# Joining the sign of decoded weights: bit operation on VectorE instead of sign and product on ScalarE and GpSimd

## Chip, core and metric

The kernel runs on one core of one Trainium2 chip. The metric is device time in microseconds, the median of several executions. The engines are called as in the profile: PE (TensorE, with its weight loads as PEld), DVE (VectorE), ACT (ScalarE), POOL (GpSimd) and SP (SyncE, which issues all of this kernel's transfers).

## What is computed

Attention over 8 batches of 8 heads (576 positions, 64 per head), in which only scores within tau of a row's maximum count, and behind it two matrix products with a gate between them:

```python
scores = scale * np.matmul(q, k.transpose(0, 1, 3, 2))
thresh = np.max(scores, axis=-1, keepdims=True) - tau
scores = np.where(scores >= thresh, scores, -1000000000.0)
...
out = np.matmul(attn, v)                     # per head; heads are joined to x, 4608 x 512
...
h = x @ w_in                                 # w_in 512 x 2048
g = h * (1.0 / (1.0 + np.exp(-h)))
return (g @ w_out).astype(np.float32)        # w_out 2048 x 512
```

The weights `w_in` and `w_out` are handed over as 64-bit floats. A 64-bit float is two 32-bit words here, a low and a top one; sign, exponent and the first 20 bits of the mantissa are in the top word.

## The kernel before, in words

Attention runs tile by tile: 128 query rows of one head against all 576 keys. For each tile PE computes scores (`scores`, L400 for the first, direct visits, L412 after), DVE takes the row maximum (L422), ACT the exponential (L429), DVE the threshold and row sum (L441, L445, L449), ACT scales (L454). The result is split into a high and a low half-precision part (ACT L463 or POOL L465, POOL L468 and L471), transposed by DMA (L481) and multiplied with v on PE (L496). In the first visits, which cover the first 256 rows of each head of batch 0, PE transposes instead (L357, L359), and L377 multiplies with v. K and q are split as well (ACT L324, L310, L315; POOL L326, L311; DVE L316). Once a batch's rows are there, units of the two matrix products are put between the attention tiles: `h_unit` (PE L530, then ACT L538, DVE L539, ACT L546, DVE L547) and `o_unit` (PE L562, ACT L572).

The weights are made once, in 32 tiles of 128 x 512, 16 of `w_in` and then 16 of `w_out`. `load_weights` has SP fetch a tile's words (L169): eight of the `w_in` tiles into parts of `gbuf`, all others into `wraw`, a pool of two buffers that are used in turn, so a load waits until all readers of the tile two before it are done. `decode_weights` turns a tile's words into 32-bit floats in `wst`:

- POOL L179 reads the top words as floats and scales them, which moves the exponent into its place but three bits to the right;
- DVE L183 shifts the words left by three, which drops the sign, and L186 joins the top three bits of the low words;
- PE L197 adds up the tile's columns in four matmuls with ones, which needs the magnitudes without sign, and for every fourth tile DVE L202 takes the maximum of the sums;
- ACT L204 takes the sign of the top words into a half-precision tile `wsg` (two buffers), and POOL L205 multiplies `wst` with it in place. POOL therefore waits for L186, for L197's reading of the tile, and for L204.

When the 16 tiles of a matrix are decoded, `pow2_scales` makes a scale from the maxima, and `split_weights` splits each tile into two half-precision parts (ACT L211, DVE L212) in place, one row of `wst` further down. Matrix products wait for these parts.

The program is written in the order of attention tiles; `W_PLAN` says at which tile each load, decode and split is put, the second group with a raised priority. A planner then sorts the instructions of each engine by priority and by its own estimate of when they are ready. Each engine works off its own queue in that fixed order. SP's queue, which issues the loads of weights, of q, k and v, and the transposes, stands still when the transfer at its head has to wait.

Of the kernel before, what the change touches and what calls it, by code (L numbers as in the profile page):

```python
# [9 lines left out]
F16 = mybir.dt.float16  # L10
BF16 = mybir.dt.bfloat16
F32 = mybir.dt.float32
F32R = mybir.dt.float32r
I32 = mybir.dt.int32
AF = mybir.ActivationFunctionType
ALU = mybir.AluOpType
# [3 lines left out]
P = 128  # L20
# [32 lines left out]
def attention_moe(  # L53
# [10 lines left out]
    nc = tc.nc  # L64
# [5 lines left out]
    stage = stage_ctx.enter_context(tc.tile_pool(name="stage", bufs=2))  # L70
# [7 lines left out]
    def bank(shape, name, own=None):  # L78
        if own is None:
            own = turn[0] = (turn[0] + 1) % turn[1]  # L80
        return ps_m.tile(shape, F32, tag=f"m{own}", name=name)
# [7 lines left out]
        out=gate, in0=tau_sb, scalar1=0.0, scalar2=0.125, op0=ALU.is_ge, op1=ALU.mult  # L89
# [3 lines left out]
        out=ntau, in0=tau_sb, scalar1=0.0, scalar2=-1.0, op0=ALU.max, op1=ALU.mult  # L93
# [55 lines left out]
    ident = const.tile([P, P], F32, name="ident")  # L149
    make_identity(nc, ident)  # L150
    wsc = {}

    w_words = (w_in.bitcast(I32), w_out.bitcast(I32))
    wraw = {}
    wps = {}
# [16 lines left out]
    def decode_weights(i):  # L172


        t = wraw.pop(i)
        low, top = t[:, :, 0], t[:, :, 1]
        w = wst[:, i + WSPARE, :]
        wbits = w.bitcast(I32)
        nc.gpsimd.tensor_scalar(  # L179
            out=w, in0=top.bitcast(F32), scalar1=2.0**-112, scalar2=1.0,  # L180
            op0=ALU.mult, op1=ALU.mult,
        )
        nc.vector.tensor_scalar(  # L183
            out=wbits, in0=wbits, scalar1=3, scalar2=None, op0=ALU.logical_shift_left
        )
        nc.vector.scalar_tensor_tensor(  # L186
            out=wbits, in0=low, scalar=29, in1=wbits,
            op0=ALU.logical_shift_right, op1=ALU.bitwise_or,
        )


        n, c = divmod(i, 4)
        if c == 0:
            wps[n] = bank([P, P], f"wps_{n}", 2)
        upper = w.bitcast(BF16).rearrange("p (c t) -> p c t", t=2)[:, :, 1]
        for j in range(4):
            nc.tensor.matmul(  # L197
                wps[n], ones, upper[:, j * P : (j + 1) * P],
                start=(c == 0 and j == 0), stop=(c == 3 and j == 3),
            )  # L200
        if c == 3:
            nc.vector.tensor_reduce(out=wmx[:, n : n + 1], in_=wps[n], op=ALU.max, axis=AX.X)  # L202
        sg = stage.tile([P, 512], F16, tag="wsg", name=f"wsg_{i}", bufs=2)
        nc.scalar.activation(sg, top.bitcast(F32), AF.Sign)  # L204
        nc.gpsimd.tensor_tensor(out=w, in0=w, in1=sg, op=ALU.mult)  # L205

    def split_weights(i):
        w = wst[:, i + WSPARE, :]
# [452 lines left out]
    for first, t0, t1, t2, hp in W_PLAN:  # L661
        for i in range(16):
            ti = t0 + i * (t1 - t0) / 16
            at(math.floor(ti - 2), pri(hp, lambda i=i + first: load_weights(i)))
            at(math.floor(ti), pri(hp, lambda i=i + first: decode_weights(i)))
        at(t1, pri(hp, scale_out if first else scale_in))
        for i in range(16):
            at(t1 + i * (t2 - t1) // 16, pri(hp, lambda i=i + first: split_weights(i)))
# [116 lines left out]
```

## Time and profile before

| | |
|---|---|
| median of 3 runs | 1275.36 us (1275.25 to 1276.07) |
| the profiled execution | 1276.61 us, its span 1274.6 us |
| PE busy | 1155.0 us, 91% of the span |
| DVE busy | 940.2 us, 74% |
| ACT busy | 869.0 us, 68% |
| POOL busy | 754.1 us, 59% |
| granted TensorE clock, mean | 0.969 |

Busy times are of one profiled execution, counted from its first to its last instruction. The sum of a forecast is made against that execution's own time; the median of the other runs lies 1.25 us below it. A share of the span mixes stages: the first 154 us, in which the weights are decoded beside the first attention tiles, look different from the rest, so the rows below separate them. A row that groups instructions gives busy time, mean duration of one, and the idle time of the engine just before them. DVE instructions overlap a little with the one behind them, so a start-to-start distance can be shorter than a duration.

### The profile page before, as it was taken

How to read it: one execution, taken by the hardware profiler on the slowest of the kernel's cores; microseconds unless marked ns; L12 is line 12 of the kernel's file. 1: busy time of each engine (PE TensorE's matmuls, PEld its weight loads, DVE VectorE, ACT ScalarE, POOL GpSimd, SP SyncE). 2: the span in 40 equal slices, each digit the busy share in tenths (PEclk: the TensorE clock that was granted, in tenths of full speed). 3: DMA queues.
4: the chain of work that ended last, by engine and by line, in shares of the span. 5: the costliest groups of instructions: out<-in, count | busy, mean ns of one | idle time of the engine just before them, and what ended most of it. 6: DMA issues, size and time to landing. Idle time of an engine off the chain costs nothing.

```text
span 1274.6 us, 27048 instructions
## 1 busy us (share of the span) xinstructions
PE 1155.0 (91%) x9400; PEld 897.5 (70%) x9400; DVE 940.2 (74%) x2339; ACT 869.0 (68%) x1793; POOL 754.1 (59%) x952
## 2 busy tenths in 40 slices
PE   5766669899899899998989999999989999999998
PEld 3544558567677677776767777787777777777777
DVE  7899997987987988868588767977597847521431
ACT  6887877787787877867478746877488747532431
POOL 5568979687788777884478608872578508300000
PEclk9886989899899999999999999999999999999999
DMA  9456778778698778782678528781687518400000
GB/s 303 133 173 165 166 135 156 153 134 179 138 158 159 149 159 154 137 166 67 140 135 151 121 75 159 141 161 50 129 158 138 111 24 139 73 15 20 6 15 19
DMA packets 363480, 158.15 MB, mean 124 GB/s; under 512 B 329552, under 2 KB 338256, under 8 KB 363344
## 3 DMA queue, kind: packets, MB, share of 16 engines
q1 hardware_dynamic: 363344, 156.43, 59.5%
q8 instruction: 74, 1.21, 0.4%
q14 instruction: 62, 0.51, 0.1%
HBM read 66.72 MB, written 9.44 MB: 60 GB/s over the span
## 4 chain that ended last, share of the span: by engine, by line
PE 47%; DVE 22%; POOL 9%; issue 9%; ACT 6%; DMA 6%; SPq 1%; POOLq 0%; ACTq 0%; DVEq 0%
PE o L562 20%; PE h L530 14%; PE s L412 6%; DVE w L441 6%; PE a L496 6%; DVE sm L422 4%; DMA wT<-hl 4%; POOL hl L468 3%; DVE qstack L316 3%; POOL hl L465 3%; DMA vraw<-in_vL 2%; ACT w L429 2%; DVE wst L212 2%; DVE gbuf L547 1%; ACT w L454 1%
## 5 line engine op out<-in xcount | busy, mean ns | idle before, releaser
L530 PE MATMUL h<-x,wst 128*128 128x288 f16 (+2 forms) x3072 | 416.2, 291 | 20.8 <-DVE gbuf L547 16.9
L562 PE MATMUL o<-gbuf,wst 128*128 128x288 f16 (+2 forms) x3072 | 398.8, 287 | 0.1
L530 PEld LDWEIGHTS <-wst 128*128 128x128 f16 x3072 | 295.0, 99 | 111.6 <-issue 29.5
L562 PEld LDWEIGHTS <-wst 128*128 128x128 f16 x3072 | 292.5, 98 | 83.7 <-issue 6.7
L468 POOL TENSOR_TENSOR hl<-w,hl 128x512 f16<-128x512 f32 x272 | 324.5, 1193 | 13.5
L465 POOL TENSOR_SCALAR hl<-w 128x576 f16<-128x576 f32 x264 | 182.8, 696 | 238.6 <-ACT w L454 127.4
L429 ACT ACTIVATE w<-s,sm 128x576 f32<-128x576 f32 x288 | 213.1, 740 | 99.8 <-DVE sm L422 32.6
L441 DVE SCALAR_TENSOR_TENSOR w<-s,sm,w 128x576 f32<-128x576 f32 x288 | 233.5, 812 | 61.9 <-ACT sm L433 28.9
L422 DVE TENSOR_REDUCE sm<-s 128x1 f32<-128x576 f32 x288 | 216.4, 752 | 70.3 <-PE s L412 66.0
L454 ACT ACTIVATE w<-w,sm 128x576 f32<-128x576 f32 x288 | 220.4, 773 | 52.1 <-DVE sm L449 50.5
L412 PE MATMUL s<-khi,qstack 128*128 128x288 f32 x608 | 157.0, 340 | 52.3 <-DVE w L441 49.1
L539 DVE SCALAR_TENSOR_TENSOR h<-th,h 128x288 f32<-128x288 f32 (+2 forms) x256 | 116.3, 456 | 81.4 <-ACT th L538 76.0
L412 PEld LDWEIGHTS s<-khi,qstack 128*128 128x128 f32 x608 | 96.1, 193 | 81.4 <-issue 46.1
L538 ACT ACTIVATE th<-h,msc 128x288 f32<-128x288 f32 (+2 forms) x256 | 127.8, 502 | 26.8 <-PE h L530 24.4
L547 DVE SCALAR_TENSOR_TENSOR gbuf<-h,gbuf 128x288 f16<-128x288 f32 (+2 forms) x256 | 115.3, 452 | 37.6 <-ACT gbuf L546 36.8
L546 ACT ACTIVATE gbuf<-h 128x288 f16<-128x288 f32 (+2 forms) x256 | 104.6, 410 | 50.9 <-DVE h L539 50.3
L496 PE MATMUL a<-wT,v 128*64 128x288 f16 (+1 forms) x1680 | 127.8, 293 | 8.3 <-DMA wT<-hl 7.1
L412 PE MATMUL s<-klo,qstack 128*128 128x288 f32 x608 | 132.9, 299 | 0.0
L326 POOL TENSOR_TENSOR klo<-kraw,khi 128x576 fp32r<-128x576 f32 x64 | 93.0, 1453 | 43.7 <-ACT khi L324 43.7
L496 PEld LDWEIGHTS <-v 128*64 128x64 f16 x1680 | 90.7, 111 | 36.0 <-issue 20.9
L412 PEld LDWEIGHTS s<-klo,qstack 128*128 128x128 f32 x608 | 99.8, 192 | 1.1 <-issue 1.1
L471 POOL TENSOR_TENSOR hl<-w,hl 128x64 f16<-128x64 f32 x272 | 99.7, 367 | 0.0
(84 smaller groups left out, 915.1 us busy)
## 6 DMA issues: line engine op xcount, KB each, us to landing
qraw<-in_qT SPq DMA_DIRECT2D x128, 144.0 KB, 3.0
kraw<-in_kT SPq DMA_DIRECT2D x128, 144.0 KB, 3.0
vraw<-in_vL SPq DMA_DIRECT2D x32, 320.0 KB, 3.8
wraw<-in_w_out SPq DMA_DIRECT2D x16, 512.0 KB, 4.2
out_t<-wst SPq DMA_DIRECT2D x56, 144.0 KB, 2.4
wT<-hl SPq DMA_TRANSPOSE x304, 3.3
gbuf<-in_w_in SPq DMA_DIRECT2D x8, 512.0 KB, 6.8
wraw<-in_w_in SPq DMA_DIRECT2D x8, 512.0 KB, 4.9
```

The costliest lines, as they stand in the source:

```text
L412: nc.tensor.matmul(s_ps[:, j, :HALF], lhs, kk[:, j * HALF : (j + 1) * HALF], start=(n == 0), stop=(n == len(seq) - 1),)
L422: nc.vector.tensor_reduce(out=negm, in_=s_ps[:, :, :HALF], op=ALU.max, axis=AX.XY, negate=True)
L429: nc.scalar.activation(wtile[t].rearrange("p (j c) -> p j c", j=2), sps[t][:, :, :HALF], AF.Exp, bias=small[t][:, 0:1],)
L441: nc.vector.scalar_tensor_tensor(out=w3, in0=s_ps[:, :, :HALF], scalar=sm[:, 1:2], in1=w3, op0=ALU.is_ge, op1=ALU.mult, accum_out=sm[:, 2:3],)
L454: nc.scalar.activation(w, w, AF.Copy, scale=r)
L465: nc.gpsimd.tensor_scalar(out=fl[:, 0:S], in0=w, scalar1=1.0, scalar2=1.0, op0=ALU.mult, op1=ALU.mult)
L468: nc.gpsimd.tensor_tensor(out=fl[:, 640:1152], in0=w[:, 0:512], in1=fl[:, 0:512], op=ALU.subtract)
L496: nc.tensor.matmul(a_ps[odd * D : (odd + 1) * D, :n], vt[:, lo_v, odd, kv, :], wT[v, b * H + 2 * p + odd][:, kw, c0 - base : c0 - base + n ...
L530: nc.tensor.matmul(ph[:, :n], wi(c, f, lo_w), x16[b, lo_x][:, c, c0 : c0 + n], start=(k == 0), stop=(k == 11),)
L538: nc.scalar.activation(th[:, :n], ph[:, :n], AF.Tanh, scale=moe_sc[b][:, 0:1])
L547: nc.vector.scalar_tensor_tensor(out=g[:, 1, :n], in0=ph[:, :n], scalar=2.0**-14, in1=g[:, 0, :n], op0=ALU.mult, op1=ALU.subtract,)
L562: nc.tensor.matmul(ps[:, :n], wo(f, d, lo_w), g[:, lo_g, :n], start=(f == 0 and k == 0), stop=(f == NF - 1 and k == 2),)
```

## The change

The sign of a tile is no longer computed as a number. One DVE instruction takes the top words, keeps bit 31 of each, and joins it with the magnitudes in `wst` by a bitwise or, in place. ACT's L204 and POOL's L205 go, and with them the tile `wsg`. The new instruction stands at the same place of `decode_weights`, behind the four matmuls that read the magnitudes and behind L202. It reads the raw top words, which L204 read before. What `wst` holds at the end is the same. (One empty line goes as well, so that lines between it and the new instruction move up by one.)

```diff
-        sg = stage.tile([P, 512], F16, tag="wsg", name=f"wsg_{i}", bufs=2)
-        nc.scalar.activation(sg, top.bitcast(F32), AF.Sign)
-        nc.gpsimd.tensor_tensor(out=w, in0=w, in1=sg, op=ALU.mult)
+        nc.vector.scalar_tensor_tensor(
+            out=wbits, in0=top, scalar=-(2**31), in1=wbits,
+            op0=ALU.bitwise_and, op1=ALU.bitwise_or,
+        )
```

## Rows read from the trace of the kernel before

**Rows 1.** Busy us (and instructions) of PE, PEld, DVE, ACT, POOL; clock; DMA
```profile
6.00:100.00 94.00, 67.59 (x335) 43.30 (x335) 87.06 (x191) 75.40 (x156) 53.72 (x51) 0.86 0.62 203
100.00:154.00 54.00, 32.35 (x230) 24.90 (x229) 51.26 (x104) 41.25 (x82) 49.39 (x50) 0.81 0.76 176
...
154.00:1274.00 1120.00, 1055.07 (x8836) 829.32 (x8836) 801.05 (x2039) 750.78 (x1555) 649.34 (x844) 0.99 0.59 115
```

**Rows 2.** Pieces of the chain of waits: start us, us, what
```profile
14.19 1.30 POOL wst L205
...
145.21 0.10 POOL wst L205
...
1108.40 21.67 PE o L562 x176
```

**Rows 3.** Instructions by line: shortest/median/longest ns, first and last start in us
```profile
L183 DVE TENSOR_SCALAR wst<-wst x32: 403/762/1375, 11.9 to 146.0; 128x512 int32<-128x512 int32 x32
...
L186 DVE SCALAR_TENSOR_TENSOR wst<-wraw,wst x24: 676/692/1827, 24.1 to 147.3; 128x512 int32<-128x512 int32 x24
...
L212 DVE SCALAR_TENSOR_TENSOR wst<-wst,i_w_sc x16: 729/1054/1906, 77.6 to 128.1; 128x512 f16<-128x512 f32 x16
...
L205 POOL TENSOR_TENSOR wst<-wst,wsg x32: 1144/1163/1682, 14.2 to 153.1; 128x512 f32<-128x512 f32 x32
```

**Rows 4.** Groups by line, 0 to 154 us: busy us, mean ns | idle before, releaser
```profile
L183 DVE TENSOR_SCALAR wst<-wst 128x512 int32<-128x512 int32 x32 | 26.5, 830 | 3.1 <-POOL wst L179 3.1
...
L186 DVE SCALAR_TENSOR_TENSOR wst<-wraw,wst 128x512 int32<-128x512 int32 x24 | 20.3, 848 | 0.0
L212 DVE SCALAR_TENSOR_TENSOR wst<-wst,i_w_sc 128x512 f16<-128x512 f32 x16 | 18.1, 1130 | 0.0
L186 DVE SCALAR_TENSOR_TENSOR wst<-gbuf,wst 128x512 int32<-128x512 int32 x8 | 8.0, 1003 | 0.0
...
L205 POOL TENSOR_TENSOR wst<-wst,wsg 128x512 f32<-128x512 f32 x32 | 40.6, 1275 | 22.4 <-PE wps L197 14.0 <-ACT wsg L204 2.3 <-issue 1.7
...
L204 ACT ACTIVATE wsg<-wraw 128x512 f16<-128x512 f32 x24 | 16.0, 665 | 5.8 <-DMA wraw<-in_w_out 4.4 <-POOL wst L205 1.5
```

**Rows 5.** Timeline, DVE and POOL: start us, us, instruction [idle before, releaser]
```profile
41.65 0.68 DVE L186 SCALAR_TENSOR_TENSOR wst<-gbuf,wst 128x512 int32<-128x512 int32 x1
42.25 0.81 DVE L441 SCALAR_TENSOR_TENSOR w<-s,sm,w 128x576 f32<-128x576 f32 x1
...
45.97 2.27 POOL L205 TENSOR_TENSOR wst<-wst,wsg 128x512 f32<-128x512 f32 x2 [9.45 <-PE wps L197]
```

**Rows 6.** Timeline, the first and the last of 18 pairs of POOL and DVE
```profile
18.89 1.16 POOL L205 TENSOR_TENSOR wst<-wst,wsg 128x512 f32<-128x512 f32 x1 [1.73 <-issue]
19.30 1.03 DVE L183 TENSOR_SCALAR wst<-wst 128x512 int32<-128x512 int32 x1
...
145.21 1.16 POOL L205 TENSOR_TENSOR wst<-wst,wsg 128x512 f32<-128x512 f32 x1
146.01 0.65 DVE L183 TENSOR_SCALAR wst<-wst 128x512 int32<-128x512 int32 x1
```

**Rows 7.** Timeline, POOL and DVE behind one line 205
```profile
107.10 1.15 POOL L205 TENSOR_TENSOR wst<-wst,wsg 128x512 f32<-128x512 f32 x1
...
108.22 1.33 POOL L468 TENSOR_TENSOR hl<-w,hl 128x512 f16<-128x512 f32 x1
...
108.46 1.64 DVE L212 SCALAR_TENSOR_TENSOR wst<-wst,i_w_sc 128x512 f16<-128x512 f32 x1
```

**Rows 8.** Waits of DVE up to 155 us: us in total, times, longest us
```profile
DVE vmx L239 <- DMA vraw<-in_vL: 5.0, 4, 3.3
DVE wst L183 <- POOL wst L179: 3.1, 4, 1.9
```

**Rows 9.** Waits of POOL and of SP's queue up to 155 us
```profile
POOL wst L205 <- PE wps L197: 14.0, 3, 9.5
...
SPq L169 <- DVE wst L186: 27.9, 12, 4.7
```

## Prediction

> **What bounds the kernel now.** The page's shares show PE as the fullest engine over the whole run, but that is an average over stages. So I went on to the busy time by stretch, where the reader should compare the columns within a row. From 154 us on, PE works 1055.07 of 1120 us: it sets the pace there. From 6 to 100 us it works only 67.59 of 94 us and from 100 to 154 only 32.35 of 54 [rows 1]. Another engine is full there: DVE is busy 87.06 and 51.26 us of these two stretches, so that from 6 to 154 us it idles 9.7 us in all. POOL is a little over half busy up to 100 us (53.72 of 94) and nearly full after (49.39 of 54) [rows 1]. The weights are decoded in just this stretch: the first line 205 starts at 14.2, the last at 153.1 us [rows 3]. A DVE queue that is almost never empty, and on which the softmax that feeds PE stands in order, is the bound of this stage.
>
> Does a delay there reach the end? The chain of waits ends in a backlog that PE works off in blocks of 21 to 24 us from 1108 us on [rows 2]. PE's order is fixed in the program, and this backlog stands behind the attention of the last batch. What the first stage loses is therefore lost at the end: PE could win back only idle time after 154 us (65 us of 1120 [rows 1]), and no row says that a late start fills it.
>
> **How full is DVE really?** Its busy time includes being held. The shortest line 183 takes 0.403 us and the mean is 0.830; line 186 takes 0.676 at the shortest against 0.848 and 1.003; line 212 takes 0.729 against 1.130 [rows 3, 4]. Over 32, 24 + 8 and 16 instructions that is 13.7 + 6.7 + 6.4 = 26.8 us above the shortest forms. The timeline shows by what: POOL runs nothing for the 9.45 us before 45.97 us, and line 186 stands at its shortest there [rows 5]; but while line 205 runs on POOL from 18.89 us for 1.16, line 183 starts at 19.30 and ends at 20.33, 0.3 us behind it, having taken 1.03 [rows 6]. I paired each long DVE instruction of these three lines with the POOL instruction that it overlaps most. 18 of them fall to line 205, the first at 19.30 and the last at 146.01 us [rows 6], 12.9 us together.
>
> **The change part by part.**
> 1. Removed from POOL: 32 of line 205, 40.6 us, mean 1.275 [rows 4]. POOL isn't the fullest engine of the stage, so this is no gain by itself; the gain is what line 205 holds DVE, at most 12.9 us. After 100 us POOL is so full that its next instruction moves up into the place: behind the line 205 of 107.10 stands line 468 at 108.22, which holds line 212 for 1.64 us [rows 7]. I therefore count 9 of the 12.9; the ends are 6, about half, and 12.9.
> 2. Removed from ACT: 32 of line 204, of which 24 took 16.0 us [rows 4]. ACT is busy 75.40 of 94 and 41.25 of 54 us [rows 1], and neither of DVE's two longest waits of the stage is for it [rows 8]. I count nothing, since DVE's own queue covers it; without that cover a tile's chain would be shorter by nothing either, because line 204 reads the raw words and can run beside lines 179 to 197. The far end is the 21 us that all 32 take at 0.665 each, if ACT were the bound.
> 3. Added to DVE: 32 bit operations. The trace has their like: line 186, the same kind of instruction on the same tile, one strided input and one in place, 128x512 words, 0.676 us [rows 3]. The instruction behind it starts 0.60 us after it (41.65 to 42.25) [rows 5]. 32 x 0.60 = 19.3 us, on the fullest engine. To this comes what POOL's remaining work holds them. Line 186 loses 6.7 / 32 = 0.21 each now, 3.2 us of it in the pairs with line 205, which leaves 0.11 each, 3.5 us. The ends are nothing and line 212's 0.40 each, 12.8 us. I take 3.5, by the row of its own kind.
> 4. A new wait. The operation rewrites the tile that line 197's four matmuls read, so DVE now waits for PE where POOL did. Behind it on DVE stand softmax and the next decode, for which PE's scores wait. POOL stands 14.0 us in three such waits, the longest 9.5 [rows 9]; that one is POOL's empty time before 45.97 us [rows 5]. A planner orders DVE's queue and may place the operation after other work. The ends are 0 and 14 us; I take 3, nearer to nothing because 29 of the 32 had no such wait.
> 5. Load buffers. Tiles outside gbuf rotate through two buffers, freed so far by lines 179, 186 and 204, then by line 179 and the added operation, which comes after PE. SP's queue already stands 27.9 us behind line 186 for such loads, with the transposes and the q and k loads behind them [rows 9]. A late load would show on DVE through POOL's line 179, for which line 183 waits 3.1 us in all [rows 8]. That is the far end of this step, and I put it inside the 3 us of step 4.
> 6. DVE's idle 9.7 us can take part of the new work. 5.0 of it are waits for v from memory [rows 8], which need not end earlier. I take 4; the ends are 0 and 9.7.
>
> The sum is 19.3 + 3.5 - 9 + 3 - 4 = +12.8 us. The profiled execution took 1276.61 us around its span of 1274.6; the median of the runs, 1275.36, lies 1.25 below it. 1276.6 + 12.8 - 1.25 gives 1288.
>
> One rule speaks against step 3. Line 186 has two inputs of 32 bits from SBUF and takes 0.676 us at its shortest [rows 3]. The Trainium skill, "Vector Engine (DVE) Microarchitecture Reference", section "Points that are easy to get wrong", puts this form of instruction at half throughput when both inputs lie in SBUF and aren't bf16. At the 1.0417 ns a column that the same page gives at full rate, half rate would add some 0.53 us to each, 17 us in all, an estimate from that page, and the sum would be +30. The trace doesn't agree: 0.676 us leaves only 0.14 beside 512 columns at full rate.
>
> **The rivals.**
> A, faster: POOL is the real limit after 100 us. For it: POOL's 49.39 of 54 us [rows 1], and line 205 as a link of the chain of waits, seven times from 14.19 to 145.21 us, 7.9 us together [rows 2]. Then all 12.9 us of holds go, the other 13.9 shrink with POOL's busy time (103 to some 63 us, 38%: 5.3), the chain drops its 7.9, and part of DVE's idle is filled as before: 19.3 + 3.5 - 12.9 - 5.3 - 7.9 - 4 = -7 us, 1268. It decides if POOL ends last after 100 us. Against it: DVE is fuller than POOL in the same stretch, 51.26 to 49.39 us [rows 1]. The Trainium skill sides with this rival in "GPSIMD Engine Reference", section "Engine selection": elementwise work with two inputs belongs on VectorE, GpSimd being about twice as slow. The trace agrees on the ratio (1.144 to 0.676 us at the shortest [rows 3]).
> B, slower than the forecast: DVE waits for PE as POOL did, 14.0 us in place of the 3, and, standing, fills none of its idle: 12.8 + 11 + 4 = +28, 1303. It decides where the operation stands at the head of DVE's queue while PE still works through scores.
> C, it cancels: all 12.9 us of holds go and all of DVE's idle is filled, 19.3 + 3.5 - 12.9 - 9.7 = 0, 1275. This needs every wait of DVE to be one that the new work can fill; half of the idle is for memory.
> That the planner sorts other instructions anew when a step costs something else is in no row. It can move each case by some us either way, and I take nothing for it.
>
> **How the numbers follow.** The forecast, +6 to +20 us around 1288, gets 0.50, because DVE's load grows by an amount that rows give. A gets 0.20, B 0.18, C 0.12. About 0.2% (2.6 us) is what a measurement of this kernel can tell from no change. Faster by more than that is A, 0.20; within it C, 0.12; slower the forecast and B, 0.68. The range 1266 to 1303 takes in A's and B's own times and leaves about 0.1 out on each side, where their further ends lie.
>
> **What would show it.** The added operation should have a mean of 0.7 to 0.9 us; above 1 us step 3 is wrong. Line 183's mean should fall from 0.83 to some 0.55; if it stays, step 1 is wrong. The last line 183, which started at 146.0 us [rows 6], should come some 13 us later, with DVE over 90% busy until then; well below 90% and earlier is A. The block that PE begins at 1108 us [rows 2] should begin later by as much; if not, later stages give time back, and the passage to the end was wrong. DVE's waits for PE at the new operation tell the forecast (about 3 us) from B (over 10).

## The result, and the profile after

The changed kernel takes 1283.85 us (median of 4 runs, 1281.78 to 1285.09) against 1275.71 before: ratio 1.0050, 95% interval 1.0027 to 1.0073, about 6 us by the ratio (the two medians lie 8.1 us apart). Run once more it came to 1.0061 (1.0039 to 1.0083), about 8 us. The change makes the kernel slower, by some 6 to 8 us. The profiled execution has a span of 1283.3 us. Lines have moved: 169, 179, 183, 186 and 197 are 168, 178, 182, 185 and 196 now, line 202 is the added operation and the column maximum is line 201.

Groups of VectorE instructions of the changed kernel up to 200 us (busy us, mean ns | idle before, releaser); rows 4 holds the same of before:

```profile
L182 DVE TENSOR_SCALAR wst<-wst 128x512 int32<-128x512 int32 x32 | 20.4, 636 | 4.7 <-POOL wst L178 4.7
L202 DVE SCALAR_TENSOR_TENSOR wst<-wraw,wst 128x512 int32<-128x512 int32 x24 | 19.9, 831 | 0.0
L185 DVE SCALAR_TENSOR_TENSOR wst<-wraw,wst 128x512 int32<-128x512 int32 x24 | 19.8, 830 | 0.0
L212 DVE SCALAR_TENSOR_TENSOR wst<-wst,i_w_sc 128x512 f16<-128x512 f32 x16 | 14.9, 935 | 0.0
...
L202 DVE SCALAR_TENSOR_TENSOR wst<-gbuf,wst 128x512 int32<-128x512 int32 x8 | 6.0, 766 | 0.0
```

The added operation has a mean of 0.831 and 0.766 us, as line 185 beside it. Line 182 fell from 0.830 to 0.636 and line 212 from 1.130 to 0.935 [rows 4]: GpSimd holds VectorE less. And the added operation has no idle time before it: VectorE did not stand waiting for PE there (only the column maximum, just ahead of it, waits 1.8 us for PE, 0.8 before).

Busy time by stretch, columns as in rows 1:

```profile
6.00:100.00 94.00, 67.75 (x346) 43.75 (x347) 84.41 (x199) 62.39 (x130) 27.24 (x29) 0.82 0.60 183
100.00:154.00 54.00, 32.60 (x237) 25.69 (x236) 49.85 (x107) 38.55 (x82) 39.36 (x43) 0.81 0.82 178
```

VectorE is no busier in these two stretches than before (84.41 and 49.85 us against 87.06 and 51.26 [rows 1]), although it has a new operation. So the work is not squeezed into the same time; it is spread. The maxima of the column sums show over what (shortest/median/longest ns, first and last start in us), first of before, then of the changed kernel:

```profile
L202 DVE TENSOR_REDUCE wmx<-wps x8: 265/278/292, 26.3 to 148.7; 128x1 f32<-128x128 f32 x8
```

```profile
L201 DVE TENSOR_REDUCE wmx<-wps x8: 274/278/292, 27.2 to 193.3; 128x1 f32<-128x128 f32 x8
```

The decode ends at 193.3 us instead of 148.7. Attention, meanwhile, is ahead: line 441, which each softmax tile passes once, ends for the 33rd time at 161.3 us instead of 171.7, for the 57th time at 242.0 instead of 253.9, and is late only at the 65th (285.5 against 277.1). PE was ahead as well at 154 us, with 583 matmuls since 6 us instead of 565 (the counts in the two rows above and in rows 1). But at 242 us it is behind, with 1035 matmuls since the start instead of 1116: the softmax of the 57th tile is early because units of the two matrix products have been put behind it (378 matmuls of lines 530 and 562 by 242.0 us, against 492 by 253.9). PE loses its lead from 200 to 230 us (columns as in rows 1, first before, then the changed kernel):

```profile
200.00:230.00 30.00, 28.59 (x250) 24.50 (x248) 22.91 (x68) 22.14 (x43) 24.72 (x34) 1.00 0.90 181
```

```profile
200.00:230.00 30.00, 22.18 (x130) 15.87 (x130) 29.84 (x62) 26.32 (x47) 29.33 (x31) 0.83 0.71 133
```

Of the matmuls in these 30 us, 90 instead of 152 are of line 562, which needs `w_out`. The splits of `w_out` (line 212) start from 199.5 to 229.3 us instead of 151.5 to 186.1, on a VectorE that is busy for 29.84 of the 30 us. Waits of PE between 200 and 260 us in the changed kernel:

```profile
PE o L562 <- DVE wst L212: 4.6, 5, 1.6
PE s L412 <- DVE w L441: 3.0, 5, 1.3
```

Before, line 562 doesn't wait for line 212 in this stretch, and PE is busy for 53.79 of the 60 us, now for 49.51. From there on a delay stays: 6.2 us at the 121st line 441 (459.1 against 452.8), and PE's backlog begins at 1117.08 us instead of 1108.40 [rows 2], 8.7 us later, which is the difference of the two spans.

```profile
1117.08 21.67 PE o L562 x176
```

**Why the decode is late.** The raw words of a tile are now free only when the sign is in, and there are two buffers. Timeline of the changed kernel, one buffer's turns (start us, us, what):

```profile
145.72 0.54 SPq L168 DMA_DIRECT2D wraw<-in_w_out  x1
...
160.18 0.35 SPq L168 DMA_DIRECT2D wraw<-in_w_out  x1
...
175.28 0.54 SPq L168 DMA_DIRECT2D wraw<-in_w_out  x1
```

```profile
155.93 1.51 DVE L185 SCALAR_TENSOR_TENSOR wst<-wraw,wst 128x512 int32<-128x512 int32 x1
159.28 0.87 DVE L202 SCALAR_TENSOR_TENSOR wst<-wraw,wst 128x512 int32<-128x512 int32 x1
...
174.22 0.68 DVE L202 SCALAR_TENSOR_TENSOR wst<-wraw,wst 128x512 int32<-128x512 int32 x1
```

The load issued at 145.72 fills a buffer; line 185 has used its low words by 157.44; the sign ends at 160.15, and 0.03 us later the next load into that buffer is issued. The sign of that tile ends at 174.90, and the next load stands at 175.28. A buffer turns once in about 15 us, so two of them let one tile through in 7.5. That is the pace of the whole of `w_out`: the last 16 tiles' line 185 starts from 79.9 to 190.8 us, 7.4 us a tile. Before, line 186 of these tiles started from 71.2 to 147.3 us, 5.1 us a tile. GpSimd shows the same from the other side; its waits up to 200 us, changed kernel:

```profile
POOL wst L178 <- DMA wraw<-in_w_out: 27.4, 11, 5.7
POOL wst L178 <- DMA wraw<-in_w_in: 20.0, 7, 15.0
POOL wst L178 <- DMA gbuf<-in_w_in: 17.6, 7, 9.5
```

Before, these were 8.0, 2.3 and 9.3 us. A GpSimd that has lost its product waits for loads.

### The profile page after: what moved, and what is told of

Its sections match the earlier page's. It is cut to its first block, busy times and chain, and to the rows that moved or that the text cites. A ratio compares the mean times of both kernels' runs of the same rounds, so it can differ in the third digit from the quotient of the medians.

```text
span 1283.3 us, 26993 instructions
## 1 busy us (share of the span) xinstructions
PE 1159.9 (90%) x9400; PEld 898.9 (70%) x9400; DVE 949.9 (74%) x2371; ACT 853.5 (67%) x1761; POOL 717.9 (56%) x920
## 4 chain that ended last, share of the span: by engine, by line
PE 44%; DVE 23%; POOL 10%; issue 9%; ACT 6%; DMA 5%; SPq 1%; POOLq 0%; ACTq 0%; DVEq 0%
PE o L562 18%; PE h L530 15%; DVE w L441 6%; PE s L412 5%; PE a L496 5%; DVE sm L422 4%; POOL hl L468 4%; DMA wT<-hl 3%; DVE qstack L316 3%; POOL hl L465 3%; ACT w L429 2%; POOL hl L471 2%; DVE wst L212 1%; DVE gbuf L547 1%; ACT w L454 1%
```

## Experiments

Two theories went in. D: the loss is the load of 32 more operations on a full VectorE, minus what taking line 205 away gives back. L: the loss is the longer hold of the raw words, which paces the decode of `w_out`. Times are given as ratios to the kernel before on the same chip, with 95% intervals, and in us as the ratio's share of 1277 us.

**The product on VectorE, the raw words freed early** (on the kernel before):

```diff
-        nc.gpsimd.tensor_tensor(out=w, in0=w, in1=sg, op=ALU.mult)
+        nc.vector.tensor_tensor(out=w, in0=w, in1=sg, op=ALU.mult)
```

> The kernel before with line 205's product moved from GpSimd to VectorE; ScalarE still takes the sign, so the raw words are released early, as before. VectorE gets 32 operations with two SBUF inputs, as in the change, and the same wait for PE. Theory L (the loss of the change comes from the raw words being held longer, so that the two load buffers pace the decode of w_out): the last column maximum comes back to 150 to 160 us and the time to 1271 to 1279 us. Theory D (the loss comes from 32 more operations on a full VectorE): 1283 us or more, as the change or worse, since ScalarE keeps its work.

1.0018 (0.9995 to 1.0041), +2 us, and the column maxima end at 163.6 us. The same load and the same place on VectorE as in the change (mean 0.879 us), without the hold: the decode ends 30 us earlier than in the change, though still 15 later than before and 4 later than L expected. The expected time of L was right at its upper end, D's was too high. The step from here to the change is 4 to 6 us, with intervals that overlap, so its size isn't certain.

**The hold alone** (on the kernel before; `held` is one column):

```diff
+    held = const.tile([P, 1], F32, name="held")
...
         nc.gpsimd.tensor_tensor(out=w, in0=w, in1=sg, op=ALU.mult)
+        nc.gpsimd.tensor_tensor(
+            out=held[:, 0:1], in0=w[:, 0:1], in1=top[:, 0:1].bitcast(F32), op=ALU.mult
+        )
```

> The kernel before, with one GpSimd operation of one column added behind line 205 of each tile that reads the raw words and the finished tile: the load buffer is held until the sign is in, and nothing else changes (32 operations of 0.1 to 0.3 us on GpSimd). Theory L: the last column maximum comes 20 to 45 us later than at 149 us, and the time rises by 4 to 12 us, to 1280 to 1288. Theory D: 1275 to 1278 us, the decode ends at 149 to 155 us.

1.0142 (1.0115 to 1.0170), +18 us, more than L expected, and the column maxima end at 236.1 us, 87 later than before, where L expected 20 to 45:

```profile
L203 DVE TENSOR_REDUCE wmx<-wps x8: 272/278/293, 25.5 to 236.1; 128x1 f32<-128x128 f32 x8
```

GpSimd's product comes later than the change's operation on VectorE, so the buffers are held longer still. The added column takes about 0.19 to 0.36 us, 32 of them some 7 us on an engine that isn't full; they don't explain an end 87 us later. Nor does attention show a fuller engine in the first stage: its 33rd softmax tile is early (150.2 us against 171.7), its 65th late (303.0 against 277.1), as in the change. A hold can cost more than the whole change.

**The load alone** (on the kernel before, behind line 186):

```diff
+        nc.vector.scalar_tensor_tensor(
+            out=wbits, in0=wbits, scalar=0, in1=wbits,
+            op0=ALU.logical_shift_right, op1=ALU.bitwise_or,
+        )
```

> The kernel before with 32 more VectorE operations of the form of line 186 (the tile joined with itself, which leaves it as it is) right behind line 186: the VectorE load of the change alone, without the wait for PE, without the longer hold, with ScalarE and GpSimd as before. Theory D: +12 to +25 us, 1288 to 1300, since line 205 still holds VectorE too. Theory L: +0 to +5 us.

1.0140 (1.0112 to 1.0168), +18 us, where D expected 12 to 25 and L at most 5. VectorE is full from 100 to 154 us (columns as in rows 1):

```profile
100.00:154.00 54.00, 26.78 (x173) 19.45 (x172) 54.00 (x98) 39.93 (x76) 42.08 (x39) 0.72 0.67 159
```

Here attention is late from the first stage on: line 441's work ends for the 33rd time at 184.1 us instead of 171.7, for the 57th at 272.6 instead of 253.9. The added operation also stands ahead of PE's reading of the tile, and the column maxima end at 182.9 us with the raw words freed as before: a late decode by itself doesn't point to the hold. So neither theory is the whole: each cause alone costs 18 us on the kernel before.

**No sign at all** (the change without its operation; the weights stay magnitudes):

```diff
-        nc.vector.scalar_tensor_tensor(
-            out=wbits, in0=top, scalar=-(2**31), in1=wbits,
-            op0=ALU.bitwise_and, op1=ALU.bitwise_or,
-        )
```

> The change without the added operation: no sign is joined on any engine, so the weights stay magnitudes. It prices what taking away lines 204 and 205 gives by itself. Both theories: faster than before; by the prediction's step 1 some 9 to 13 us, 1262 to 1267. If it gives less than 4 us, line 205's holds were not on the path.

0.9898 (0.9870 to 0.9927), -13 us.

**No product on GpSimd, ScalarE's sign kept but unused** (the kernel before without line 205; the weights stay magnitudes):

```diff
-        nc.gpsimd.tensor_tensor(out=w, in0=w, in1=sg, op=ALU.mult)
```

> The kernel before without line 205: no product on GpSimd, the sign is taken on ScalarE but used nowhere, so the weights stay magnitudes. It parts ScalarE's share from GpSimd's in the run without any sign (12.3 us below the kernel before). By the prediction's step 2 ScalarE's work is covered and this run is within 3 us of that one, 1263 to 1269 us. The rival: ScalarE's 21 us of work are worth several us, and this run is at 1270 us or above.

0.9862 (0.9835 to 0.9889), -18 us, somewhat below the 1263 to 1269 us that were expected. No cost of ScalarE's 32 signs shows: with them the kernel is, if anything, faster than without. Line 205 is worth 13 to 18 us. The two intervals overlap, so it isn't certain that the run with more work is the faster one. If it is, the planner's new order is the likely reason, and can move a time by a few us.

**The operation cut to one column** (the change; the other weights stay magnitudes), and the change itself on the same chip:

```diff
-            out=wbits, in0=top, scalar=-(2**31), in1=wbits,
+            out=wbits[:, 0:1], in0=top[:, 0:1], scalar=-(2**31), in1=wbits[:, 0:1],
```

> The change with the added operation cut to one column of its tile (the other weights stay magnitudes): its place on VectorE, its wait for PE and its hold of the raw words stay, its load goes from 0.68 to 0.15 us or less. Theory D (the load of 32 operations is the whole price, 18 to 20 us): 1262 to 1270 us, with 32 small operations some 2 to 3 us above the run without any sign; the last column maximum may still come late. Theory L (wait and hold cost several us of their own): 1272 us or more.

> The change itself once more, beside the run with one column on the same chip. Both theories: 4 to 10 us above the kernel before, 1281 to 1288 us.

One column: 0.9996 (0.9976 to 1.0017), no difference from the kernel before; the change: 1.0061 (1.0039 to 1.0083), +8 us. D expected 1262 to 1270 us and fell: with nearly all of its load gone, the operation still costs 12 to 13 us over the run without any sign. Its column maxima end at 174.7 us, at 141.5 without any sign. The rest of the operation's length, 0.77 (this run of the change) to 0.81 us (the first) instead of 0.27 in the mean, costs 8 us more.

```profile
L202 DVE SCALAR_TENSOR_TENSOR wst<-wraw,wst 128x1 int32<-128x1 int32 x24 | 7.0, 296 | 0.2 <-PE wps L196 0.2
```

**Which part of the one column costs: the hold, or its place and wait?** Two runs take the hold away and leave the small operation. First, the kernel before with line 205 moved to VectorE and cut to one column, so that ScalarE frees the raw words early (the other weights stay magnitudes):

```diff
-        nc.gpsimd.tensor_tensor(out=w, in0=w, in1=sg, op=ALU.mult)
+        nc.vector.tensor_tensor(out=w[:, 0:1], in0=w[:, 0:1], in1=sg[:, 0:1], op=ALU.mult)
```

> The kernel before with line 205 moved to VectorE and cut to one column (the other weights stay magnitudes): like the change with one column, a small VectorE operation that waits for PE at the same place, but ScalarE still takes the sign from the raw words, so they are free before PE has read the tile. Theory L (the 12 us between no sign and the change with one column are the hold of the raw words): last column maximum at 125 to 150 us, 1262 to 1269 us. The rival (they are the small operations and their waits for PE): within 3 us of the run with one column, 1274 to 1280 us.

Second, the one-column kernel with three buffers, for which `gbuf` gives room:

```diff
-GB = 17
+GB = 16
...
-            t = stage.tile([P, 512, 2], I32, tag="wraw", name=f"wraw_{i}", bufs=2)
+            t = stage.tile([P, 512, 2], I32, tag="wraw", name=f"wraw_{i}", bufs=3)
```

> The change with one column, with three load buffers (and the ring of 16 parts of gbuf that makes room, which cost nothing clear by itself): the hold stays, its price as a pace of the loads should go. Theory L: last column maximum at 140 to 160 us instead of 175, 1264 to 1272 us. The rival (small operations and waits): 1274 to 1281 us.

Freed early: 0.9909 (0.9889 to 0.9930), -12 us; three buffers: 0.9933 (0.9914 to 0.9953), -9 us. Both are clear of the one column's 0.9996, and the column maxima end at 137.5 and 138.7 us:

```profile
L202 DVE TENSOR_REDUCE wmx<-wps x8: 267/278/283, 25.0 to 137.5; 128x1 f32<-128x128 f32 x8
```

```profile
L201 DVE TENSOR_REDUCE wmx<-wps x8: 274/280/291, 23.7 to 138.7; 128x1 f32<-128x128 f32 x8
```

So of the one column's 12 to 13 us the hold is 8 to 11, shown by two different edits; place, wait and the small operations themselves leave 1 to 5.

**Three buffers at full length, and its control** (the change with the edit above; the control has the ring of 16 and two buffers):

> The change with three load buffers for the raw words instead of two (room from a ring of 16 instead of 17 parts of gbuf, as in its control). Theory M (three parts: -13 us for the work taken off GpSimd, +18 for VectorE's load, +2 to +5 for the longer hold of the raw words): the last column maximum comes at 155 to 170 us instead of 194, and the time is 2 to 6 us below the control with two buffers. Theory D (VectorE's load is all that is left, the hold only shifts the decode without a price): less than 1 us from the control.

> The change with a ring of 16 instead of 17 parts of gbuf, two load buffers: the control for the run with three. Both theories: 1282 to 1292 us, since the first unit of a matrix product may have to wait for the ring; the decode of the weights as in the change, last column maximum at 185 to 200 us.

Three buffers: 1.0038 (1.0023 to 1.0052); control: 1.0058 (1.0037 to 1.0079). The column maxima end at 159.3 instead of 191.6 us, as theory M, which adds up the three parts, expected, but the time falls by only some 2.5 us, and the intervals overlap. That VectorE is the next limit under the full load is likely but not shown: from 100 to 154 us its busy time rises from 50.35 (control) to 52.48 us, yet it is 53.53 in the run with one column freed early, which is 12 us faster than the kernel before. Attention is level with the kernel before up to the 57th softmax tile (254.6 us against 253.9), so the loss of 200 to 230 us is gone. What is left of the change's price arises behind that (279.6 against 277.1 at the 65th, 459.5 against 452.8 at the 121st); from what, wasn't followed up. The ring of 16 costs nothing that can be told from the change.

**The operation at a higher priority** (the change):

```diff
-        nc.vector.scalar_tensor_tensor(
...
+        with tc.high_priority(offset=300):
+            nc.vector.scalar_tensor_tensor(
...
```

> The change with the added operation at a priority 300 higher, so that the planner puts it ahead of other VectorE work as soon as PE has read the tile; the raw words are freed earlier. Theory M: the last column maximum comes at 155 to 185 us and the time is 1 to 5 us below the change, 1278 to 1283. Theory D: no difference from the change beyond 2 us, or slower, since softmax stands behind the operation.

1.0014 (0.9998 to 1.0029), about 5 us below the change and level with the kernel before, as is the product on VectorE (1.0018). M's time came out, but by luck, not for the reason that was expected: the column maxima still end at 191.5 us. Beside the profile of the second run of the change it is level at the 65th softmax tile (282.0 against 282.2 us) and gains only behind that (453.5 against 457.5 at the 121st, 1276.0 against 1281.0 in the span), where no weights are decoded any more. Both theories missed the place: the gain lies in later work. That the planner ordered this work anew is likely, but what it is in that order wasn't followed up.

## Why the prediction held, and where its steps were off

The direction, the range and the forecast case held: +12.8 us was forecast, 1288 us, and +6 to +8 were measured, inside the case's +6 to +20. That the sum came this near is partly luck: it gave line 205's removal too little, VectorE's load at its place in the change and the waiting for PE too much, and the hold nothing of its own; these errors partly cancel. Point by point:

- **VectorE as the bound of the first stage** was right. The load alone costs 18 us, and the forecast's terms for it, 19.3 + 3.5 - 4, are 18.8. In the change the operation's length costs only 8, and 14 where the hold is gone. The operation takes 0.77 to 0.83 us, inside the 0.7 to 0.9 that were named, and what it loses to GpSimd's holds is some (0.831 - 0.667) x 24 + (0.766 - 0.676) x 8 = 4.7 us by its own shortest forms in the trace, 3.5 in the sum. The operation takes 0.667 us for 512 columns at its shortest, 0.27 more than the one-input shift of the same tile (0.400). The rule of the Trainium skill that the prediction cites ("Vector Engine (DVE) Microarchitecture Reference", section "Points that are easy to get wrong"), read there as half of the full rate that the page gives, isn't borne out by this.
- **Step 1 was too small.** 9 us were taken, with 12.9 as the most. The runs without line 205 give 13 and 18. On VectorE itself the holds of the three old lines shrink in the change to (636 - 400) x 32 + (830 - 676) x 24 + (789 - 672) x 8 + (935 - 727) x 16 ns = 15.5 us from 26.8, that is by 11.3: fewer holds move to the next GpSimd instruction than I had assumed, though line 183's mean fell to 0.636 us and not to 0.55. By the same sum they shrink by 10.0 us without any sign and by 15.2 without the product, which is most of the 13 and 18. What the other 2 to 3 us are isn't shown; line 205 as a link of the chain of waits [rows 2], which only rival A had counted, is one candidate.
- **Step 2, ScalarE for nothing,** was right, to within what the two runs can tell.
- **Step 4, 3 us of waiting for PE,** did not happen: the added operation has no idle time before it. The planner put it late enough. That is where rival B failed.
- **Step 5 was priced from the wrong row.** I took line 183's 3.1 us of waiting as the far end of what a longer hold can do. That row tells how much the loads cost as they are, not how near the two buffers are to setting the pace. The row that would have told it is the 27.9 us that SP's queue already stood behind line 186 [rows 9]: a load issued the moment that a reader is done means that the buffer's turn is the pace, and each us added to a turn is added to every second tile. By itself the hold costs 18 us on the kernel before and 8 to 11 with the short operation; with the full operation some 2.5 to 5.5 are left, probably because VectorE's load then hides it.
- **Where the time shows** was wrong. I had the whole first stage late by 13 us, with the last line 183 at 159. It started at 187.3 us, 41 us later, and up to 154 us PE was ahead, not late. The loss appears at 200 to 230 us, where PE's order reaches units that need `w_out`. The passage to the end held: 8.3 us at 285 us, 6.2 at 459, 8.7 at 1117 us and in the span.

Put together from the runs: -13 (no sign) + 12.5 (the operation as one column, of which 8 to 11 are the hold) + 8 (its length) gives about +8. Without the hold: -12 (one column, freed early) + 14 (its length) gives +2, and -9 (one column, three buffers) + 14 gives +5. The length costs 14 us where the hold is gone and 8 where it is there, so the two causes overlap and don't add: both ask for the same stretch before PE needs `w_out`.

Three things stay open: the exact share of the hold in the change, since its 2.5 to 5.5 us are no wider than the intervals of the runs that it is the difference of; where the 5 us come from that three buffers leave; and what is gained behind 280 us in the run with the higher priority. That last gain, of 5 us as well, is a warning for every other difference of this size here.

## What to carry to other kernels

When an operation moves to another engine, list what it reads last, not only where it runs: an operand that had been freed early may now be held to the end of a chain, and with two buffers the loads then go at the pace of that chain. A queue that already waits, load by load, for the release of a buffer says that the buffers set the pace. A longer hold then delays the end of the loads by what it adds to a turn, times the number of turns: here 2 x (7.4 - 5.1) = 4.6 us a turn and about 7.5 turns for 16 tiles, 35 of the 45 us by which the decode ended later (most of the others are its later start). How much of that is lost time depends on when the tiles are needed. And weigh both sides of an engine's relief: 32 products on GpSimd cost 13 to 18 us here; 32 bit operations of some six tenths of their length cost 8 to 18 us on the fuller VectorE, and with the longer hold the whole came out dearer than the products.

## What was not expected of the hardware

Taking GpSimd's 32 products away shortened VectorE's own one-input shift most: its median went from 0.762 to 0.418 us with a shortest form of 0.403 and 0.400. Ten of the 32 had been standing behind line 205 in the pairs of which rows 6 shows the first and the last.

```profile
L182 DVE TENSOR_SCALAR wst<-wst x32: 400/418/1376, 12.5 to 187.3; 128x512 int32<-128x512 int32 x32
```

It isn't line 205 alone that holds the shift. In the kernel before, 18 of the 32 shifts took over 0.46 us, and each of them ends 0.28 to 0.29 us behind the end of the GpSimd instruction that it overlaps most, whichever line that is. Here it is line 468, which ends at 102.86 us:

```profile
101.70 1.16 POOL L468 TENSOR_TENSOR hl<-w,hl 128x512 f16<-128x512 f32 x1
101.77 1.38 DVE L183 TENSOR_SCALAR wst<-wst 128x512 int32<-128x512 int32 x1 [1.91 <-POOL wst L179]
```

So these shifts stand until GpSimd's instruction is done: one of them takes what was left of that instruction when it started, and 0.28 us more.
